# A kernel of chunked attention and grouped experts: one more GpSimd drain between the loop over units and the last scatter

## The chip, the cores and the metric

The kernel runs on one core of a Trainium2 chip. The metric is the device time of one execution in microseconds. Three runs of the kernel before took 676.79, 677.04 and 678.67 us; the median is 677.04 us.

## The reference

The input is q, k and v of shape (8, 8, 576, 64). Attention is computed within chunks of 64 positions, so each head of each batch has nine independent 64 by 64 softmaxes. The result is rearranged to 4608 tokens of 512 features. A router with two levels picks one of 4 groups and then one of 4 experts in that group for every token, and a token goes through that one expert only:

```python
g_idx = np.argmax(x @ w_group, axis=1)
...
e_idx = np.argmax(xg @ w_expert[g], axis=1)
...
h = np.maximum(xg[mask_e] @ w1[g, e], 0.0)      # 512 -> 1024
ye = h @ w2[g, e]                               # 1024 -> 512
out[tok_idx] = (g_w * e_w)[:, None] * ye        # the two softmax weights
```

Everything is float32.

## The kernel before

**First part.** Attention is worked off in 36 tiles of 128 tokens. Each finished tile of tokens, with its token number and its gate in two more columns, is scattered by GpSimd into a buffer `xs` in device memory, at a row that the routing gave, so that the tokens of one expert lie together (line 505, four scatters for each group of four tiles; the last group at line 1321).

**Second part.** It runs over units: a unit is up to 256 tokens of one expert. The number of units, `nu`, and each unit's kind, rows and expert are known only at run time; the vector engine writes them into a table `tb`, and every engine reads them into registers with `val`, which is a load from `tb` (line 700). All of the second part stands in one block (line 718) in which each engine has a stream of its own, written out by hand. The streams meet only at semaphores: an engine runs its stream in order, and a wait holds everything behind it on that engine.

For each unit TensorE transposes the gathered tokens, multiplies by the first weights (`L1p`, `L1s`, `L1h`) and then by the second (`L2`, line 849). The vector engine scales the result by the gate into `yb` (`YE`, line 1050), and adds 1 to the semaphore `Y`. The kind `k` of a unit says how many rows it has; with `k > 1` there are two halves and two scatters, otherwise one.

**GpSimd's stream** (from line 1295) is the one the change touches. Before the loop it issues the last four scatters to `xs`, the first gathers, and the two scatters of unit 0. In each pass of its loop (line 1341, 22 passes in the profiled execution) it waits until TensorE has read the gathered tokens, copies two columns of them (`carry2`, lines 1311 and 1312), gathers the next tokens from `xs` (`gather`, line 1306, or a dummy of four bytes at line 1356), and then issues the scatters of a unit to the output (`scatter`, line 1317; where the unit has one half, a dummy of four bytes at line 1364). `scatter` waits for `Y` first (line 1315, recorded at 1316), so that GpSimd stands at that wait until the vector engine has written `yb`.

Behind the loop the stream loads the last unit's kind (line 1367) and issues the last unit's scatter or scatters under a semaphore of their own, `Se`. In both branches a `gp.drain()` comes next, then the wait for `Se`, then the end of the stream:

```python
scatter(2 * nu, 0, io, sem="Se")
...
gp.drain()          # line 1377, the branch that ran
W("Se", 16)
gp.sem_inc(S["Z"], 1)
```

The block is opened with `no_gpsimd_drain=True` (lines 717 and 718), so that its end adds no drain of GpSimd; it does add one for the other engines. GpSimd's sequencer reads instructions ahead of the engine: registers, branches and the drain are executed by the sequencer (`POOLq` in the profile), copies and DMA issues by the engine (`POOL`).

Of the kernel before, what the change touches and what calls it, by code (L numbers as in the profile page):

```python
# [91 lines left out]
def moe_kernel(tc, q, k, v, w_group, w_expert, w1, w2, cst, out):  # L92
# [3 lines left out]
    with ExitStack() as ctx:  # L96
# [103 lines left out]
        with ExitStack() as c1:  # L200
# [393 lines left out]
            def load_wg(_):  # L594
                nc.vector.tensor_copy(tri, cs[:, C_TRI:C_TRI + P])
                nc.gpsimd.tensor_copy(identr, ident)
                nc.sync.dma_start(wg[:, :, 0:G], w_group.rearrange("(c p) g -> p c g", p=P))
                for g in range(G):
                    nc.sync.dma_start(wg[:, :, 4 + 4 * g:8 + 4 * g], w_expert[g].rearrange("(c p) e -> p c e", p=P))
# [93 lines left out]
        def by_turns(eng, u, f):  # L693
            with eng.If((u & 1) == 0):
                f(io_[0], io_[1])
            with eng.Else():
                f(io_[1], io_[0])

        def val(eng, at, lo, hi):
            return nc.values_load(tb[0:1, ds(at, 1)], engines=[eng.engine], min_val=lo, max_val=hi,  # L700
                                  skip_runtime_bounds_check_because=WHY)
# [15 lines left out]
        with tc.tile_critical(no_gpsimd_drain=True):  # L717
            with nc.Block(no_gpsimd_drain=True) as blk:
# [322 lines left out]
                def _(ve):  # L1041
# [133 lines left out]
                    with ve.Fori(1, nu) as u:  # L1175
# [40 lines left out]
                        def out_(io, _):  # L1216
                            def free():
                                W("Is", 2 * u)
                                W("Sc", 32 * u)

                            with ve.If(k > 1):
                                free()
                                W("L2", 2 * u + 1)
                                YE(0, io).then_inc(S["Y"], 1)
                                with ve.If(k > 2):
                                    W("L2", 2 * u + 2)
                                    YEh(u, 1, 1, io)
                                with ve.Else():
                                    W("L2", 2 * u + 2)
                                    YE(1, io).then_inc(S["Y"], 1)  # L1230
                                    ve.sem_inc(S["M"], 1)
                            with ve.Else():
                                with ve.If(k == 1):
                                    free()
                                    W("L2", 2 * u + 2)
                                    YEh(u, 0, 2, io)
                                with ve.Else():
                                    free()
                                    W("L2", 2 * u + 2)
                                    ve.sem_inc(S["M"], 1)  # L1240
                                    YE(0, io).then_inc(S["Y"], 2)
# [53 lines left out]
                def _(gp):  # L1295
# [45 lines left out]
                    with gp.Fori(1, nu - 1) as u:  # L1341
# [23 lines left out]

                        by_turns(gp, u, unit)
                    k = val(gp, nu + (KIND - 1), 0, 3)

                    def last_out(io, _):
                        scatter(2 * nu, 0, io, sem="Se")  # L1370
                        with gp.If(k > 1):
                            scatter(2 * nu, 1, io, sem="Se")
                            gp.drain()
                            W("Se", 32)
                            gp.sem_inc(S["Z"], 1)
                        with gp.Else():
                            gp.drain()
                            W("Se", 16)
                            gp.sem_inc(S["Z"], 1)
# [28 lines left out]
```

## Time and profile before

| what | us |
|---|---|
| median of three runs | 677.04 |
| profiled execution, its own time | 672.6 |
| its span, first to last instruction | 671.0 |
| TensorE busy | 622.2 (93%) |
| vector engine busy | 394.5 (59%) |
| scalar engine busy | 325.4 (49%) |
| GpSimd busy | 171.6 (26%) |
| DMA queue `q0`, issued by GpSimd | 10864 packets, 33.64 MB |

The span is the time from the first to the last instruction in the trace; the execution's own time has 1.6 us around it. "Busy" is the time in which an engine's instructions ran; the sequencers' work (`POOLq` and the like), the drains among it, is not counted in it. `PEclk` is TensorE's granted clock as a share of full speed.

### The profile page before, as it was taken

What the parts mean: (1) busy time and instruction counts of PE and PEld (TensorE: products, weight loads), DVE (VectorE), ACT (ScalarE), POOL (GpSimd) and SP (SyncE); (2) the same over time, 40 slices, a digit from 0 to 9 for tenths busy, and PEclk for the clock granted to TensorE, in tenths of its full rate; (3) what the DMA queues carried; (4) which work ended last, traced back from release to release, by engine and by line L of the source; (5) the groups of instructions that cost most, each with busy time, mean ns of one, the idle gap of its engine ahead of it and who ended that gap; (6) DMA issues with size and microseconds to landing.
All of it is one profiled execution on the core that took longest, in us unless ns stands there. A gap on an engine that the chain in (4) does not pass through costs nothing.

```text
span 671.0 us, 16852 instructions
## 1 busy us (share of the span) xinstructions
PE 622.2 (93%) x5866; PEld 554.5 (83%) x5867; DVE 394.5 (59%) x731; ACT 325.4 (49%) x450; POOL 171.6 (26%) x261
## 2 busy tenths in 40 slices
PE   5899999988787799999999999999999999999992
PEld 4788888876676699887988988988899988898981
DVE  2568887876578584522749757472722778863220
ACT  3687888887453263311547635342523374551110
POOL 1001212338315221312235322232211323222110
PEclk9899999999798899999999999999999999999997
DMA  9989999999702796711448876281630867921010
GB/s 209 233 190 227 272 256 242 266 281 253 224 34 95 272 371 207 292 47 43 157 157 294 320 285 234 102 286 66 219 125 31 288 221 285 319 105 48 24 39 16
DMA packets 116339, 128.12 MB, mean 191 GB/s; under 512 B 48894, under 2 KB 83966, under 8 KB 116288
## 3 DMA queue, kind: packets, MB, share of 16 engines
q1 hardware_dynamic: 105424, 93.76, 48.3%
q0 software_dynamic: 10864, 33.64, 14.5%
q8 instruction: 37, 0.61, 0.4%
q14 instruction: 14, 0.11, 0.1%
HBM read 106.23 MB, written 21.93 MB: 191 GB/s over the span
## 4 chain that ended last, share of the span: by engine, by line
PE 83%; DVE 5%; ACT 5%; issue 3%; SPq 2%; DMA 1%; POOLq 0%; DVEq 0%; ACTq 0%
PE py L849 27%; PE ph L834 18%; PE lgk L834 6%; PE ph L818 5%; PE o L333 4%; PE sc L297 4%; PE tp L276 4%; PE py L866 2%; PE pxt L734 2%; PE tp L362 2%; PE tp L320 2%; SPq L249 1%; ACT qT L280 1%; PE ph L780 1%; PE lgk L369 1%
## 5 line engine op out<-in xcount | busy, mean ns | idle before, releaser
L834 PE MATMUL ph<-xt,w1h 128*128 128x256 f32 x672 | 100.7, 287 | 5.5 <-issue 5.5
L989 ACT ACTIVATE hth<-ph 128x512 fp32r<-128x512 f32 x43 | 25.7, 598 | 153.8 <-PE ph L834 151.4
L834 PEld LDWEIGHTS ph<-xt,w1h 128*128 128x128 f32 x672 | 91.1, 195 | 7.3 <-issue 6.4
L1317 POOL DMA_INDIRECT out_dram<-xl,io x37 | 41.7, 1127 | 151.7 <-DVE xl L1050 135.0
L1064 DVE TENSOR_TENSOR w2l<-w2r,w2h 128x1024 fp32r<-128x1024 f32 x60 | 69.5, 1220 | 6.1 <-ACT w2h L1004 4.6
L1060 DVE TENSOR_TENSOR w1l<-w1r,w1h 128x2048 fp32r<-128x2048 f32 x28 | 63.0, 2290 | 13.1 <-ACT w1h L976 11.5
L849 PE MATMUL py<-w2h,hth 128*128 128x512 f32 x264 | 67.7, 398 | 0.0
L849 PE MATMUL py<-w2l,hth 128*128 128x512 f32 x264 | 65.3, 389 | 0.0
L849 PE MATMUL py<-w2h,htl 128*128 128x512 f32 x264 | 65.2, 389 | 0.0
L1050 DVE TENSOR_SCALAR xl<-py,io 128x512 f32<-128x512 f32 x33 | 24.7, 749 | 68.0 <-PE py L849 68.0
L1083 DVE SCALAR_TENSOR_TENSOR htl<-ph,hth 128x512 fp32r<-128x512 f32 x40 | 27.4, 688 | 59.8 <-ACT hth L989 59.4
L849 PEld LDWEIGHTS py<-w2l,hth 128*128 128x128 f32 x264 | 49.6, 188 | 10.6
L849 PEld LDWEIGHTS py<-w2h,htl 128*128 128x128 f32 x264 | 49.6, 188 | 10.3
L849 PEld LDWEIGHTS py<-w2h,hth 128*128 128x128 f32 x264 | 47.6, 188 | 10.1 <-ACT hth L1035 0.9
L834 PE MATMUL ph<-xt,w1l 128*128 128x256 f32 x336 | 55.1, 286 | 0.5 <-DVE w1l L1060 0.5
L976 ACT CAST w1h<-w1r 128x2048 fp32r<-128x2048 f32 x28 | 52.0, 1903 | 1.9 <-issue 1.8
L980 ACT CAST w2h<-w2r 128x2048 fp32r<-128x2048 f32 x28 | 52.3, 1925 | 0.0
L505 POOL DMA_INDIRECT xs<-x,pos x24 | 23.7, 988 | 98.4 <-DVE rc L341 65.3
L280 ACT COPY qT<-tp 64x512 f32<-64x512 f32 x68 | 42.5, 625 | 12.3 <-PE tp L276 11.6
L834 PEld LDWEIGHTS ph<-xt,w1l 128*128 128x128 f32 x336 | 47.2, 195 | 0.7 <-DVE w1l L1060 0.7
L333 PE MATMUL o<-va,pT 64*64 64x65 f32 x1152 | 42.9, 223 | 5.2 <-issue 2.7
L276 PE MATMUL tp<-cs,qk 128*128 128x128 f32 x272 | 43.2, 283 | 3.6 <-DMA qk<-in_k_dram 1.9
(269 smaller groups left out, 1111.9 us busy)
## 6 DMA issues: line engine op xcount, KB each, us to landing
w1r<-in_moe_w_dram SPq DMA_DIRECT2D x30, 1024.0 KB, 5.3
w2r<-in_moe_w_dram SPq DMA_DIRECT2D x30, 1024.0 KB, 7.3
xgr<-xs POOLq DMA_DIRECT2D x38, 257.0 KB, 5.0
va<-in_v_dram SPq DMA_DIRECT2D x32, 256.0 KB, 7.5
qk<-in_q_dram SPq DMA_DIRECT2D x11, 512.0 KB, 6.7
qk<-in_k_dram SPq DMA_DIRECT2D x11, 512.0 KB, 7.7
w1r<-in_moe_w_dram POOLq DMA_DIRECT2D x2, 1024.0 KB, 8.5
w2r<-in_moe_w_dram POOLq DMA_DIRECT2D x2, 1024.0 KB, 8.9
```

The source lines that it names most:

```text
L276: nc.tensor.transpose(pt[:, hp, :], st["q", n // 4][:, z, 2 * hp + x], ident)
L280: (nc.vector.tensor_copy if z and not a else nc.scalar.copy)(to[:, a], pt[64 * a:64 * a + 64])
L333: nc.tensor.matmul(o[HALF[c], x, hp * W:hp * W + W], lhsT=pT[HALF[c], hp, HALF[x]], rhs=s["va"][HALF[c], 2 * hp + x], start=True, stop=True)
L818: m = pe.matmul(ph[n], a_[:, c, 0:P], w_[:, c, n * 512:(n + 1) * 512], start=(i == 0), stop=(i == 11))
L834: m = pe.matmul(ph[f // 2][:, f % 2 * 256:f % 2 * 256 + 256], w_[:, c, f * P:(f + 1) * P], a_[:, c, :], start=(i == 0), stop=(i == 11))
L849: m = pe.matmul(py[j], a_[:, f, half[j]], w_(b, f), start=(i == 0), stop=(i == 23))
L976: lambda b, s, j: ac.copy(wt[b][0][:, s], w1r[j]), K1)
L980: lambda b, s, j: ac.copy(wt[b][2 + j], w2r[j]), K2)
L1060: lambda b, s, j: ve.tensor_sub(wt[b][1][:, s], w1r[j], wt[b][0][:, s].bitcast(F32)), K1, js)
L1064: m = ve.tensor_sub(wt[b][4 + 2 * j + i], w2r[j][:, 2 * i:2 * i + 2], wt[b][2 + j][:, 2 * i:2 * i + 2].bitcast(F32))
L1083: ve.scalar_tensor_tensor(out=htl()[:, 2 * b:2 * b + 2, :], in0=ph[b].rearrange("p (f t) -> p f t", f=2), scalar=0.0, in1=hth()[:, 2 * b:2 ...
L1317: gp.indirect_dma_start(out, bass.IndirectOffsetOnAxis(ap=io[:, j, 0:1].bitcast(I32), axis=0), yb[:, j, :], None, bounds_check=N - 1, oob_ ...
```

## The change

One call is added to GpSimd's stream: a drain between the load of the last unit's kind and the wait that opens the last unit's scatter. The drains that follow the last scatter, in both branches, stay where they are. No other stream is changed, no semaphore value, no transfer and no buffer.

```diff
                         by_turns(gp, u, unit)
                     k = val(gp, nu + (KIND - 1), 0, 3)
+                    gp.drain()
 
                     def last_out(io, _):
                         scatter(2 * nu, 0, io, sem="Se")
```

## Rows read from the trace of the kernel before

**Rows 1.** Chain of waits from 655 us: start us, us, what.

```profile
654.92 2.73 PE py L849 x12
...
657.80 0.76 DVE xl L1050
...
659.38 1.04 POOLq L1377
```

**Rows 2.** Line 1377: queue or engine, operation, ns min/median/max, first and last start.

```profile
L1377 POOLq DRAIN  x1: 9778/9778/9778, 659.4 to 659.4; - x1
```

**Rows 3.** GpSimd instructions from 645 us: start us, us, engine, line, operation, idle before.

```profile
646.91 0.99 POOL L1317 DMA_INDIRECT out_dram<-xl,io  x1 [4.35 <-DVE xl L1050]
659.44 0.98 POOL L1317 DMA_INDIRECT out_dram<-xl,io  x1 [11.54 <-DVE xl L1050]
```

**Rows 4.** DMA issues from 640 us: count, us to landing.

```profile
out_dram<-xl,io POOLq DMA_INDIRECT x3, 2.7
```

**Rows 5.** Windows near the end: us, busy by engine, PEclk, DMA share, GB/s.

```profile
661.00:662.00 1.00, 0.00 (x0) 0.00 (x0) 0.00 (x0) 0.00 (x0) 0.00 (x0) 1.00 0.66 254
662.00:669.00 7.00, 0.00 (x0) 0.00 (x0) 0.00 (x0) 0.00 (x0) 0.00 (x0) 0.52 0.00 0
```

**Rows 6.** Line 1392, the start of the program.

```profile
L1392 POOLq DRAIN  x1: 184/184/184, 0.5 to 0.5; - x1
```

**Rows 7.** Line 1403, the end of the program.

```profile
L1403 POOLq DRAIN  x3: 34/47/162, 669.6 to 670.7; - x3
```

**Rows 8.** Line 718, the end of the block that holds all streams.

```profile
L718 PEldq DRAIN  x1: 3448/3448/3448, 654.2 to 654.2; - x1
L718 DVEq DRAIN  x1: 441/441/441, 658.2 to 658.2; - x1
```

**Rows 9.** GpSimd groups by line, whole span: count, busy us, mean ns, idle.

```profile
L1317 POOL DMA_INDIRECT out_dram<-xl,io x37 | 41.7, 1127 | 151.7 <-DVE xl L1050 135.0 <-DVE xl L1056 16.7
...
L555 POOL DMA_DIRECT2D xg0r<-xs x2 | 1.2, 577 | 7.8 <-DMA xs<-x,pos 7.4 <-issue 0.4
```

**Rows 10.** GpSimd groups by line from 558.4 us.

```profile
L1317 POOL DMA_INDIRECT out_dram<-xl,io x9 | 9.2, 1021 | 46.7 <-DVE xl L1050 40.8 <-DVE xl L1056 5.9
L1306 POOL DMA_DIRECT2D xgr<-xs x7 | 4.1, 581 | 5.1 <-POOL ion L1312 3.1 <-issue 2.0
...
L1356 POOL DMA_DIRECT2D xgr<-xs x3 | 1.6, 539 | 0.2
L1364 POOL DMA_DIRECT2D word<-xs x2 | 1.1, 560 | 0.0
```

**Rows 11.** Line 1321, the last scatters ahead of the loop.

```profile
L1321 POOL DMA_INDIRECT xs<-xl,pos x4: 959/975/2852, 208.4 to 212.2; - x4
```

**Rows 12.** Line 1317, the scatters to the output.

```profile
L1317 POOL DMA_INDIRECT out_dram<-xl,io x37: 980/1034/2972, 254.1 to 659.4; - x37
```

**Rows 13.** GpSimd instructions from 362 us.

```profile
364.02 2.74 POOL L1317 DMA_INDIRECT out_dram<-xl,io  x1 [3.82 <-DVE xl L1050]
```

**Rows 14.** GpSimd instructions from 551 us.

```profile
555.35 2.97 POOL L1317 DMA_INDIRECT out_dram<-xl,io  x1 [2.77 <-DVE xl L1050]
```

**Rows 15.** Line 700 from 640 us: the load of k.

```profile
L700 POOLq TENSOR_LOAD <-tb x1: 292/292/292, 647.1 to 647.1; - x1
```

**Rows 16.** Line 1299 from 645 us: a register step for the wait.

```profile
L1299 POOLq FUSED_REGOPS  x1: 43/43/43, 647.7 to 647.7; - x1
```

**Rows 17.** Window between the last two scatters.

```profile
647.90:657.80 9.90, 9.72 (x49) 7.64 (x47) 1.98 (x3) 2.75 (x5) 0.00 (x1) 1.00 0.07 26
```

**Rows 18.** Line 1312, the second copy of the carried columns.

```profile
L1312 POOL COPY io<-ion x22: 186/1188/2310, 247.9 to 636.8; 128x2 f32<-128x2 f32 x22
```

## The prediction

> **What bounds the kernel now.** I read the page's table of busy time first (TensorE 93%), then the chain of waits, then the timeline of GpSimd, because the change stands in its stream. Up to 657.65 us the chain is TensorE's matmuls without a gap of note; nothing in the change touches those. Then comes a tail: the vector engine scales the last result (657.80 to 658.56), GpSimd is released, and the chain's last piece is the drain of line 1377 [rows 1]. The chain counts only 1.04 us of that drain, but the line's own row says 9778 ns from 659.38 us on, so it ends at 659.38 + 9.78 = 669.16 [rows 2]. The span ends at 671.0, 1.84 us later. So about 10 us of the 671 belong to one drain with nothing beside it: it is the bound of this stage, and a stage of 1.5% of the span is all that this change can reach.
>
> What does this drain wait for? The scatter in front of it runs on GpSimd from 659.44 for 0.98 us, to 660.42 [rows 3], and its data land 2.7 us after its start, at 662.14 [rows 4]. The windows agree: the DMA engines are busy in 661 to 662 (share 0.66), and idle from 662 to 669, with no engine at work either [rows 5]. So the drain outlasts GpSimd's last instruction by 8.74 us and the landing by 669.16 - 662.14 = 7.02 us. Those 7.02 us are the sum at stake.
>
> Is it a fixed price of a GpSimd drain? No: the drain at the start of the program, before any DMA, takes 184 ns [rows 6], and the three that come at the end of the program, within 1.6 us behind the long one and with no DMA between, take 34, 47 and 162 ns [rows 7]. Other engines' drains last as long as their last work (441 ns for the vector engine, which ends with its scaling; 3.45 us for TensorE) [rows 8]. So GpSimd's long drain is paid for DMAs issued since the last drain, and here that is since the start of the program: 137 of them, in eleven groups by line, the largest and smallest of which are shown [rows 9]. There is a second sign that GpSimd keeps books on its DMAs and settles them late. Of its 137 issues three are far longer than their like: 2852 ns where the median of that line is 975 [rows 11], and 2.74 and 2.97 us [rows 13, 14] where the median is 1.03 [rows 12]. The excess is 1.88, 1.71 and 1.94 us, at 212, 364 and 555 us, as if old entries were settled in lumps when room runs out. Since the last of these, 9 + 7 + 3 + 2 = 21 more were issued [rows 10], so between 21 and 137 entries lie behind the long drain.
>
> **The change part by part.** It adds one instruction to one sequencer and moves nothing.
>
> *The added drain.* The load of k ends at 647.1 + 0.3 = 647.4 us [rows 15]; there the drain starts. GpSimd's engine is still issuing the second-last scatter, until 646.91 + 0.99 = 647.90 [rows 3], and its data land at 646.91 + 2.7 = 649.6 [rows 4]. If the drain then pays the same 7.02 us for 136 or 20 old entries, it ends at 656.6. Behind it on GpSimd's sequencer wait only the branch on the turn and a register step, which now end at 647.7, some 0.35 us after the load [rows 15, 16]; they would end at 657.0. The next instruction is the wait for `Y`, which is not met before the vector engine's end at 658.56 [rows 1]. So the added drain lies beside TensorE's work with 1.6 us to spare, and costs nothing. If that cover were gone, each us beyond it would cost one us. Nobody else waits for GpSimd there: its engine has no instruction between 647.90 and 659.44 [rows 3], all gathers are issued before, and the DMA queues are not held by a sequencer that waits.
>
> *The last drain.* It starts at 659.38 as before, but only one DMA was issued since the drain ahead of it. The wait for `Se` behind it can't be met before the landing at 662.14, so the drain can give back 7.02 us at most, whatever it costs: the lower end of the sum. The upper end is the old length: it gives back nothing. No row shows a GpSimd drain behind exactly one DMA. The nearest rows are those with none behind them, 34 to 184 ns [rows 6, 7], and these stand at the short end; a price for each entry, from the long drain itself, is 7.02/137 = 0.05 us to 7.02/21 = 0.33 us. I take 0.2 us, so that the drain ends at 662.14 + 0.2 = 662.34.
>
> *The sum.* 669.16 - 662.34 = 6.8 us given back, 0 us paid. Behind the drain the barrier and the end of the program keep their 1.84 us. The profiled execution took 672.6 us by its own time, span 671.0 and 1.6 around it, so it would take 665.8. The runs' median of 677.04 is 4.4 above the profiled execution; since the tail stands behind TensorE's last matmul, I carry the 6.8 us over as they are: 670.2 us.
>
> A rule of the Trainium skill speaks against this: PSUM — Partial Sum Buffer, Engine vs sequencer instructions, says that a drain waits for the engine to go fully idle. By that alone the long drain would have ended with GpSimd's last instruction at 660.42, the trace has 8.74 us more, and an added drain would change nothing: 677.0 us. The measured length decides that the rule is short of something here, but not of what; that is the third case below.
>
> **The rivals.**
>
> *One lump.* The settling has a price for each pass and not for each entry, so that one entry costs as much as many. The excess of the three long issues, 1.71 to 1.94 us whatever was due, speaks for it [rows 11 to 14]; that 7.02 us is nearly four times as much speaks against it. The last drain would end at 662.14 + 1.9 = 664.0, 5.1 us are given back, and the median would be 671.9 us.
>
> *The change doesn't shorten the last drain.* The 7 us belong to the newest scatter or to any queue that isn't empty, and are due again behind one DMA; the three short drains follow no DMA at all, so they can't exclude this. For it: between 662 and 669 nothing at all moves [rows 5], as with a fixed wait, and settling at the pace of the long issues would take far less than 7 us for 21 entries. Old entries would then be worth one such pass at most: 0 to 1.9 us given back, 675.1 to 677.0 us, most likely 677.0, for the added drain is hidden as worked out above. Against it: such a fixed wait leaves the long issues unexplained.
>
> *Slower.* GpSimd's settling is slowed by the engines that work beside it, so that the added drain ends too late. The last drain has the chip for itself; the added one has the vector engine at work for 1.98 us and the scalar engine for 2.75 us of its time [rows 17], and GpSimd's copies show what company can do to it: the same copy takes from 186 to 2310 ns [rows 18]. If the drain stood still through all of that, it would end at 656.6 + 4.7 = 661.3, the wait would be reached at 661.7, and the last scatter would start 661.7 - 658.56 = 3.1 us late. It decides from 1.6 us on. With a last drain as long as ever the median would be 680.2 us; with a short one it would still be 3.7 us under the median of before. So this rival needs two things at once. Against it: the drain has no tile to read or write.
>
> By the Trainium skill (SBUF — State Buffer, SBUF: two separate sides), only the vector engine can lock GpSimd out, and only while one of its instructions holds the shared port. By that the standstill is at most the 1.98 us, and the lateness 0.4 us, 677.4 us with a long last drain; no row here shows a drain beside such an instruction.
>
> **How the numbers follow.** A difference of under 0.3%, 2.0 us, can't be told from none here. The forecast (last drain short, 670.2) has 0.66, one lump (671.9) 0.12, no shorter last drain (675.1 to 677.0) 0.16, slower (680.2) 0.06. The first two and none else are faster by over 0.3%: 0.78; the third is within it, 0.16; the fourth slower, 0.06. For the range: the lowest sum is 677.04 - 7.02 = 670.0; runs of one kernel lie up to 1.9 us apart (676.79 to 678.67), and with 1.4 of these below the sum the range begins at 668.6. Upward the first two cases hold 0.78, so it takes in half of the third, to 676.1.
>
> **What would show it.** In the changed kernel's trace: a drain on the new line, starting near 647.4 us and 7 to 10 us long, ended before the vector engine's last scaling; the last scatter issued as before, some 0.9 us after that scaling; and the drain of the last branch 2.8 to 3.1 us long where it took 9.78. A last drain of 4.6 us is the lump, one of 9 us or more the third case. A new drain of under 1 us, with the last one unchanged, would say that the newest scatter carries the price. The prediction is wrong if the last drain stays above 6 us, or if the new one ends behind the scaling.

## The result, and the profile after

The changed kernel takes 669.38 us in the median of 14 runs, the kernel before 675.36 us in the median of 14: ratio 0.9914, 95% interval 0.9889 to 0.9939. That is faster by more than 0.3%, by 5.98 us between the medians. The forecast was 670.2 against 677.04, ratio 0.990, with 0.78 on faster; it holds.

The profile shows the difference in one place. Its span fell from 671.0 to 664.0 us, with one instruction more:

```profile
span 664.0 us, 16853 instructions
```

The chain of waits (start us, us, what) reaches the last drain at the same moment as before, 659.37 against 659.38 [rows 1]. All the work ahead of the tail stands where it stood:

```profile
654.91 2.73 PE py L849 x12
...
657.79 0.76 DVE xl L1050
...
659.37 1.02 POOLq L1378
```

The two drains of the changed kernel, line 1368 (new) and line 1378 (line 1377 of before, [rows 2]); columns: operation, ns min/median/max, first and last start:

```profile
L1368 POOLq DRAIN  x1: 9165/9165/9165, 647.4 to 647.4; - x1
...
L1378 POOLq DRAIN  x1: 2867/2867/2867, 659.4 to 659.4; - x1
```

The new one starts at 647.36 us and ends at 647.36 + 9.17 = 656.5 us; the last one ends at 659.37 + 2.87 = 662.24, where it ended at 669.16 before: 6.92 us earlier. GpSimd's timeline has its two scatters where [rows 3] has them, and nothing between:

```profile
646.88 0.99 POOL L1317 DMA_INDIRECT out_dram<-xl,io  x1 [4.35 <-DVE xl L1050]
659.43 0.97 POOL L1317 DMA_INDIRECT out_dram<-xl,io  x1 [11.56 <-DVE xl L1050]
```

The register step behind the new drain, at 647.7 before [rows 16], now waits for its end, and is done 1.6 us ahead of the end of the vector engine's last scaling (658.55):

```profile
L1299 POOLq FUSED_REGOPS  x1: 43/43/43, 656.9 to 656.9; - x1
```

The windows at the end (columns as in [rows 5]) show what went: the data land in 661 to 662 as before, and then there are 2 us of program end in place of 9.

```profile
661.00:662.00 1.00, 0.00 (x0) 0.00 (x0) 0.00 (x0) 0.00 (x0) 0.00 (x0) 0.50 0.61 234
662.00:664.00 2.00, 0.00 (x0) 0.00 (x0) 0.00 (x0) 0.00 (x0) 0.00 (x0) 0.50 0.00 0
```

### The profile page after: what moved, and what is told of

It is laid out like the page before. It is cut to its first block, busy times and chain, and to the rows that moved or that the text cites. A ratio compares the mean times of both kernels' runs of the same rounds, so it can differ in the third digit from the quotient of the medians.

```text
span 664.0 us, 16853 instructions
## 1 busy us (share of the span) xinstructions
PE 624.3 (94%) x5866; PEld 556.6 (84%) x5867; DVE 395.3 (60%) x731; ACT 325.2 (49%) x450; POOL 169.8 (26%) x261
## 4 chain that ended last, share of the span: by engine, by line
PE 83%; ACT 5%; DVE 5%; issue 3%; SPq 2%; DMA 1%; POOLq 0%; DVEq 0%; ACTq 0%
PE py L849 27%; PE ph L834 18%; PE lgk L834 6%; PE ph L818 5%; PE o L333 4%; PE sc L297 4%; PE tp L276 4%; PE py L866 2%; PE pxt L734 2%; PE tp L362 2%; PE tp L320 2%; SPq L249 1%; ACT qT L280 1%; PE ph L780 1%; PE lgk L369 1%
## 5 line engine op out<-in xcount | busy, mean ns | idle before, releaser
L849 PEld LDWEIGHTS py<-w2l,hth 128*128 128x128 f32 x264 | 49.6, 188 | 10.6
```

The costliest lines, as they stand in the source:

```text
L849: m = pe.matmul(py[j], a_[:, f, half[j]], w_(b, f), start=(i == 0), stop=(i == 23))
```

## The experiments

Open after this were the price's law, whether it needs a drain at all to come due, and why the long issues [rows 11 to 14] exist. Two measures of a drain's price are used below, and each place names its own: from the end of GpSimd's last issue ahead of it (or from the drain's own start, where that came later), and from the last landing of the DMAs ahead of it. A profiled execution's front part varies by several us from run to run (in three profiles of kernels that are the same up to there, the added drain starts at 642.8, 647.4 and 649.5 us), so spans of single profiles are not compared to a us; the drains' own rows are.

### Three drains, earlier

```diff
                     W("X", 16 * NG)
+                    gp.drain()
...
                         by_turns(gp, u, unit)
+                        with gp.If(u == 4):
+                            gp.drain()
+                        with gp.If(u == 16):
+                            gp.drain()
```

> The kernel before with three drains put in GpSimd's stream: behind the last scatter to xs (42 DMAs issued by then), at the end of pass 4 (22 more) and at the end of pass 16 (48 more); the last drain then has 25. Each drain's price is its end less the landing of the last DMA ahead of it. Theory A, a price for each DMA since the last drain, 7.02/137 = 0.051 us: 2.1, 1.1, 2.5 and 1.3 us, so the last drain ends at 663.4 us or thereabouts and the span is some 5.7 us shorter at its end. Theory B, a price for each DMA since the last long issue, 7.02/21 = 0.33 us: under 0.4 us at 42 (a long issue has just been paid), 7 us at 22, 8 us at the end. Theory C, about 7 us whenever anything older than the newest scatter is due: 7 us each time.

Measured: the four drains (lines 1324, 1369, 1371 and the last, 1382; columns as above).

```profile
L1324 POOLq DRAIN  x1: 3502/3502/3502, 218.4 to 218.4; - x1
...
L1369 POOLq DRAIN  x1: 3279/3279/3279, 319.1 to 319.1; - x1
...
L1371 POOLq DRAIN  x1: 6186/6186/6186, 535.5 to 535.5; - x1
...
L1382 POOLq DRAIN  x1: 3855/3855/3855, 661.5 to 661.5; - x1
```

The first drain had everything landed, so its 3.50 us are pure price for 42 DMAs: 0.08 us each, not 0.05. The other three met their landings, and took 0.95, 2.01 and 1.07 us behind them, for 22, 48 and 25 DMAs; theory A had 1.1, 2.5 and 1.3. Theory B (under 0.4 us at the first, 8 at the last) and theory C (7 us each time) are out. Theory A has the right shape, but no single slope: twice as much for each DMA where everything had landed as behind a landing. The long issues stood at the 42nd, 75th and 116th DMA as before, though drains had been at the 64th and 112th.

### One drain in the middle of the loop

```diff
                         by_turns(gp, u, unit)
+                        with gp.If(u == 11):
+                            gp.drain()
```

> The kernel before with one drain at the end of pass 11 of the loop, when 92 DMAs have been issued; the last drain then has 45. Theory A: 92 x 0.051 = 4.7 us behind the landing at pass 11, and 45 x 0.051 = 2.3 us at the end, so that the last drain ends 4.7 us earlier than before. Theory B: 17 DMAs since the long issue of the 75th, 5.7 us; at the end between 1 and 15 us, by where the next long issue falls. Theory C: 7 us both times, and no gain.

```profile
L1368 POOLq DRAIN  x1: 8725/8725/8725, 429.6 to 429.6; - x1
...
L1379 POOLq DRAIN  x1: 4777/4777/4777, 656.9 to 656.9; - x1
```

From the end of GpSimd's last issue ahead of them (430.7 and 657.9 us) these are 7.6 us for 92 DMAs and 3.75 us for 45: again 0.08 us each. Behind the landing, as the expectation counts, the first took 6.2 us (the landing is at 432.1), where theory A had 4.7 and theory C 7: a clear miss for A's slope. The last drain ends 2.0 us behind its landing (656.96 + 2.7 = 659.7), for 2.3 expected by A and 7 by C.

### No drain behind the last scatter

```diff
                         with gp.Else():
-                            gp.drain()
                             W("Se", 16)
```

(and in the other branch the same.)

> The kernel before without the drain behind its last scatter: the stream ends with the wait for the landing alone. If the price is a debt of the DMAs (theories A to C), the first drain of the program's end, 47 ns before, takes about 7 us, and the span stays at 671 us within 0.3. If it belongs to the drain's own place and nobody else has to pay it, the span falls to about 664 us, with no drain at all behind the loop.

The drains of the program's end, line 1401 here:

```profile
L1401 POOLq DRAIN  x3: 46/162/8733, 663.1 to 672.6; - x3
```

The price doesn't vanish: the first drain of the program's end, 47 ns before [rows 7], takes 8733 ns. It starts at 663.1 us, behind the landing and the barrier, and so has neither beside it: the span is 672.9 us for 671.0, where no change within 0.3 us was expected. It is a debt of the DMAs, as A to C have it, but the expected 7 us were 8.7.

### The added drain on the path

```diff
                     def last_out(io, _):
+                        W("Y", 2 * nu + 1)
+                        gp.sem_inc(S["Z"], 1)
+                        gp.drain()
                         scatter(2 * nu, 0, io, sem="Se")
```

> The kernel before with the added drain moved onto the path: behind the wait for the vector engine's last scaling, ahead of the last scatter. By then all 136 DMAs have landed for 9 us. If the settling begins only when a drain asks for it (theories A to C), it takes its 7 us there, 658.6 to 665.6, the scatter starts at 666.5, the last drain takes 2.8 us, and the span is 671 us, as before: what the change gains is the cover alone. If old entries settle themselves with time, the drain is short, under 1 us, and the span is about 665 us. If the price runs from GpSimd's last instruction and not from the landing, it is 8.7 us and the span 672.7 us.

```profile
L1372 POOLq DRAIN  x1: 8652/8652/8652, 659.5 to 659.5; - x1
...
L1380 POOLq DRAIN  x1: 2869/2869/2869, 669.0 to 669.0; - x1
```

The vector engine's last scaling, and GpSimd's last scatter with the idle time of its engine ahead of it (columns as in [rows 3]):

```profile
658.61 0.75 DVE L1050 TENSOR_SCALAR xl<-py,io 128x512 f32<-128x512 f32 x1 [3.70 <-PE py L849]
...
669.02 0.97 POOL L1317 DMA_INDIRECT out_dram<-xl,io  x1 [20.37 <-issue]
```

The third case of what was expected: 8.65 us, though GpSimd's engine had been idle for 10.8 us (since 669.02 - 20.37 = 648.65) and all 136 DMAs had landed 9 us before. So time alone settles nothing, and the price doesn't run from the landing. The last drain is as short as in the changed kernel (2.87 us), and yet nothing is gained: it ends at 668.97 + 2.87 = 671.84, 12.4 us behind the start of the first, and the span is 673.6 us. During the 8.65 us no engine and no DMA works (columns as in [rows 5]):

```profile
659.48:668.13 8.65, 0.00 (x0) 0.00 (x0) 0.00 (x0) 0.00 (x0) 0.00 (x0) 0.66 0.00 0
```

In the changed kernel the same 136 cost 8.66 us from the end of GpSimd's last issue, 647.86 to 656.52, with the vector engine busy for 1.98 us of them and the scalar engine for 2.75:

```profile
647.86:656.52 8.66, 8.64 (x45) 7.08 (x44) 1.98 (x3) 2.75 (x5) 0.00 (x1) 1.00 0.08 30
```

Company cost the drain nothing there, so the rival that came out slower has no ground.

### The price by itself

The drain of the last experiment, and behind it groups of extra DMAs whose landings are waited for:

```diff
+                        for n, full in ((8, False), (32, False), (8, True), (24, True)):
+                            for i in range(n):
+                                ...
+                            W("Q", 16 * made)
+                            gp.sem_inc(S["Z"], 1)
+                            gp.drain()
```

> A measurement of the price by itself, at the end of the kernel before where nothing else runs: behind the wait for the last scaling a drain, then 8 DMAs of four bytes, 32 of four bytes, 8 of 128 rows of 256 bytes and 24 of these, each group followed by a wait for all its landings and a drain (the extra data go to buffers that are no longer used; the last scatter follows). The four drains of the earlier runs with least beside them, counted from GpSimd's last issue, took 2.33 us for 22 DMAs, 2.83 for 25, 3.75 for 45 and 8.65 for 136. Theory A, a price for each DMA, about 1.1 us + 0.055 us each whatever its size: 8.65, then 1.5, 2.9, 1.5 and 2.4 us. Theory D, a price for each row or packet that was moved: 8.65, then under 1.3 us for both groups of four bytes, and 1.5 and 2.4 us for the groups of 128 rows. Theory C, a lump of some 7 us: refuted by the earlier runs already.

The first drain, and then the four groups in order (one line of the kernel, in four windows):

```profile
L1372 POOLq DRAIN  x1: 8652/8652/8652, 658.7 to 658.7; - x1
...
L1387 POOLq DRAIN  x1: 700/700/700, 673.1 to 673.1; - x1
...
L1387 POOLq DRAIN  x1: 2651/2651/2651, 691.7 to 691.7; - x1
...
L1387 POOLq DRAIN  x1: 691/691/691, 700.7 to 700.7; - x1
...
L1387 POOLq DRAIN  x1: 1997/1997/1997, 716.0 to 716.0; - x1
```

Eight DMAs of four bytes cost 700 ns and eight of 32 KB cost 691: the size counts for nothing, and theory D is out. The slope is (2651 - 700)/24 = 81 ns for each DMA, and 700 - 8 x 81 = 50 ns are left, the price of an empty drain [rows 7]. So price = 0.05 us + 0.081 us for each DMA since the last drain; the 1.1 us + 0.055 us that was expected had too large a start and too small a slope. It gives 3.45 us for 42 (3.50 measured), 3.70 for 45 (3.75) and 7.50 for 92 (7.6). For 136 it gives 11.1 us, and 8.65 were measured: as if 30 had been settled before.

### A drain in every pass

```diff
                         by_turns(gp, u, unit)
+                        gp.drain()
```

> The kernel before with a drain at the end of every pass of the loop, 22 in all. Theory A: 4 to 6 DMAs each time, so each drain ends within 1.5 us of the issue or just behind the landing, some 2 to 5 us after the last issue, while GpSimd has 2.6 to 11 us to spare before its next work; the last drain ends 0.1 us behind its landing, and the span is that of the changed kernel, 664 us within 1.5. If the drains get into the gathers' way, the span is over 668 us. The three issues of 2.7 to 3.0 us at the 42nd, 75th and 116th DMA stay where they are, as three drains ahead of them did not move them.

```profile
L1367 POOLq DRAIN  x22: 2556/3930/9746, 254.8 to 644.5; - x22
...
L1378 POOLq DRAIN  x1: 2857/2857/2857, 657.1 to 657.1; - x1
```

The first in the loop had 52 DMAs to settle and took 4.33 us from the last issue, where the price list has 4.26. Behind it, the drains in the loop wait for landings and then take 0.21 to 0.22 us for four DMAs; that is a little more than half of the 0.05 + 4 x 0.081 = 0.37 us that a quiet one would take. The last drain is as short as in the changed kernel. The span is 661.8 us, under the 662.5 at which the expected range began, but by less than the front part varies. The long issues stayed. The same kernel was then timed:

> The kernel with a drain in each pass, now timed: the last drain again 0.1 us behind its landing, and the others beside TensorE's work, so that the ratio to the kernel before is 0.990, as the changed kernel's; over 0.995 if the drains hold up the gathers.

Ratio to the kernel before 0.9912 (0.9877 to 0.9947), not to be told from the change (0.9914): 22 drains beside TensorE's work cost nothing that can be measured within that interval.

### The early drain alone, and the change again

```diff
                     k = val(gp, nu + (KIND - 1), 0, 3)
+                    gp.drain()
...
                         with gp.Else():
-                            gp.drain()
                             W("Se", 16)
```

> The changed kernel without the drain behind the last scatter: the drain behind the loop alone. Theory A: the wait for the landing ends the stream 0.1 us earlier than the drain did, and the first drain of the program's end has one landed DMA to settle, 1.1 us in place of 0.05: the span is up to 1 us longer than the changed kernel's, ratio to the kernel before 0.990 to 0.994. If one landed DMA costs nothing, 0.1 us shorter: ratio 0.990.

> The changed kernel as it is, on the same chip as the run without its last drain: 6.9 us less than the kernel before at the tail, ratio 0.990, span ends 1.8 us behind the last drain.

The early drain alone has a ratio of 0.9931 (0.9906 to 0.9955), the change on the same chip 0.9918 (0.9889 to 0.9946); the intervals overlap, so which is better can't be told. In the first, the program's end (line 1402) pays for the one landed DMA:

```profile
L1368 POOLq DRAIN  x1: 9165/9165/9165, 642.8 to 642.8; - x1
...
L1402 POOLq DRAIN  x3: 46/142/162, 658.0 to 659.1; - x3
```

142 ns where 47 to 53 stand otherwise: 0.09 us for one DMA, as the price list has it (0.081). Up to 1 us had been thought possible. The change again:

```profile
L1368 POOLq DRAIN  x1: 9165/9165/9165, 649.5 to 649.5; - x1
...
L1378 POOLq DRAIN  x1: 2879/2879/2879, 661.5 to 661.5; - x1
```

None of the versions beats the change by more than can be measured; what the last drain now costs behind the landing, 0.09 us, is all that would be left to gain.

### Where 30 of 136 went

One drain at the end of pass 15, ahead of the long issue of the 116th DMA; in a second kernel at the end of pass 18, behind it:

```diff
                         by_turns(gp, u, unit)
+                        with gp.If(u == 15):
+                            gp.drain()
```

> The kernel before with one drain at the end of pass 15, behind 108 DMAs. The quiet groups gave 0.05 us + 0.081 us for each DMA (8: 0.70, 32: 2.65, 24: 2.00), which also fits 42 (3.50) and 92 (7.60), but gives 11.1 us for 136, where 8.65 were measured: as if some 30 of the 136 were settled already. Reading E, the long issue of the 116th DMA settled them: this drain ahead of it pays for all 108, 8.8 us from the last issue, and the last drain for 29, 0.05 + 0.04 x 29 = 1.2 us behind its landing or less. Reading F, no more than some 106 can be due at a time: 8.65 us here too; E and F part in the next run.

```profile
L1368 POOLq DRAIN  x1: 9933/9933/9933, 509.4 to 509.4; - x1
...
L1379 POOLq DRAIN  x1: 4022/4022/4022, 657.6 to 657.6; - x1
```

The last issue ahead of the drain (columns as in [rows 3]):

```profile
509.38 1.02 POOL L1317 DMA_INDIRECT out_dram<-xl,io  x1 [4.36 <-DVE xl L1050]
```

The drain ends at 519.3, 8.9 us behind that issue (509.38 + 1.02 = 510.4): all 108 are due (8.80 by the price list), more than the 8.65 us that reading F allows. The margin is small, 0.25 us; the last drain, 1.24 us behind its landing for 1.2 expected, says that all 29 DMAs behind the first are due.

> The kernel before with one drain at the end of pass 18, behind 120 DMAs, four after the long issue of the 116th. Reading E: some 30 of them settled by that issue, 90 left, 7.3 us from the last issue. Reading F, never more than 106 due: 8.65 us. Without any settling: 9.8 us. The last drain has 17 DMAs: 0.05 + 0.04 x 17 = 0.7 us behind its landing.

```profile
L1368 POOLq DRAIN  x1: 8998/8998/8998, 570.6 to 570.6; - x1
...
L1379 POOLq DRAIN  x1: 3537/3537/3537, 657.8 to 657.8; - x1
```

This drain met a busy stretch: its last DMA, the dummy of line 1364, was issued at 570.94 and landed 4.9 us later, at 575.9,

```profile
L1364 POOL DMA_DIRECT2D word<-xs x1: 560/560/560, 570.9 to 570.9; - x1
...
DMA to landing us min/median/max: 4.9/4.9/4.9
```

so its 8.06 us from the last issue match none of the three expected numbers (7.3 by E, 8.65 by F, 9.8 without any settling). They are still an upper bound: a drain that waited for nothing would pay 8.06 us for 99 DMAs, so at most 99 of the 120 were due, and F, with 106, is out. How many there were is read from what is left behind the landing, a reading found only afterwards: 570.56 + 9.00 = 579.56, 3.7 us later. Behind a landing the other drains took 0.21 us for 4 DMAs, 0.95 for 22, 1.07 for 25, 1.24 for 29, 2.01 for 48 and 0.75 for 17 (here, at the end), which is 0.05 + 0.041 us each, half of the price. By that 3.7 us are some 90 DMAs, 120 less 30: reading E. So some 30 DMAs were settled between the 108th and the 120th, where the long issue lies. That this issue does the settling is an inference; where a drain had come before it, it was as long as ever (2.97 us) and the DMAs behind that drain were all still due.

## Why the prediction was right, by its own steps

**The bound of the stage** was right: the tail is one drain, and its end moved by 6.92 us where 6.8 were forecast. The medians moved by 5.98 us, with an interval from 4.1 to 7.5 us (675.36 times 1 less the ratio's bounds), and the 6.92 lie in it.

**The added drain beside TensorE's work** was right to 0.1 us: forecast 647.4 to 656.6, measured 647.36 to 656.5, the next step ready by 656.9, 1.6 us of cover unused. That the cover is what pays was shown by taking it away: with the drain behind the wait, the time from the end of the last scaling to the end of the last drain is 671.84 - 659.36 = 12.5 us, where the kernel before takes 669.16 - 658.56 = 10.6 and the changed one 662.24 - 658.55 = 3.7.

**The last drain** was forecast at 2.8 to 3.1 us and took 2.87. Its part behind the landing is 0.09 us in place of the 0.2 taken; the range for each entry, 0.05 to 0.33 us, held the measured 0.081.

**The size of the debt** was taken wrongly, without harm: I read 7.02 us behind the landing, but the price runs from the end of GpSimd's last issue, or from the drain's start where that is later, and is 8.65 us. In the kernel before and in the changed one the landing comes some 1.75 us behind the end of that issue, so both readings end at the same time: that the added drain's end came out right to 0.1 us is luck in this step. In the two kernels where the drain begins after the landing the readings part, and there the 7 us of my expectation were missed by 1.7 us (no drain behind the last scatter) and 1.65 us (the drain on the path). At least half of the price follows the landing, which shows where the backlog is short or the landing late.

**The second sign**, the three long issues, was read wrongly. I took them for old entries settled in lumps. The one at the 42nd DMA settled nothing (all 42 were due behind it), nor did that at the 75th (92 and 108 all due), and drains don't move or shorten them. Only between the 108th and the 120th did some 30 entries go, most likely at the 116th, and what the excess of 1.7 to 1.9 us buys elsewhere stays open. The conclusion stood on the first sign, the short drains [rows 6, 7], and that sign was good.

**The rivals.** One lump would have shown as a last drain of 4.6 us; it took 2.87, and the price list has no lump but 0.05 us. The case without a shorter last drain is refuted by the same row. The slower case needed company to slow the drain: it took 8.66 us beside the other engines, and 8.65 with none of them at work. The rule of the Trainium skill (PSUM — Partial Sum Buffer, Engine vs sequencer instructions), a drain that waits for an idle engine, does not cover what GpSimd's drain costs: it took 8.65 us on an engine that had been idle for 10.8.

## What to carry to other kernels

A drain of GpSimd pays for every DMA that GpSimd issued since its last drain, 0.081 us each here (of 136, some 30 had been settled), whatever its size and however long ago it landed, and the program's end collects what nobody drained before. So drain once where GpSimd waits anyway, shortly before its last DMAs and with more idle time ahead than the debt is long (here 10.7 us for 8.65). Whether the drain behind the last DMA stays made no difference that could be measured here, since the program's end asks the same 0.09 us for one DMA. Look for such a debt in the sequencer's rows: the table of busy time doesn't count it.

## What the runs showed of the hardware that was not expected

- The price is for a DMA and not for its bytes: 700 ns for eight of four bytes, 691 ns for eight of 32 KB.
- Issues at a fixed count are long whatever the drains do: the 42nd, 75th and 116th took 2.7 to 3.0 us in every profile, also with 22 drains in the loop. In the kernel of the price list, which issues 209, none behind the 116th did.
- A drain with everything landed pays 0.05 + 0.081 us for each DMA; one that meets the landing pays at least 0.05 + 0.041 us for each behind it (4: 0.21, 17: 0.75, 22: 0.95, 25: 1.07, 29: 1.24, 48: 2.01).
